# Moving the cast of the next rows behind the fourth eviction, one weight set for three expert tiles, and twelve weight pieces split early

## The chip, the cores and the metric

The kernel runs on one core of one Trainium2 chip. The metric is the device time of the core in microseconds (us). A core has TensorE (PE; its weight loads are listed apart as PEld), VectorE (DVE), ScalarE (ACT), GpSimd (POOL) and SyncE (SP), which here issues most DMAs. They run their own instruction streams and wait for each other on semaphores.

## The reference, cut to what matters

The kernel computes a spectral mixing layer and then a mixture of experts with one expert per token.

```python
# x: 8 sequences of 2496 tokens, 256 wide, float32
X = np.fft.rfft(x, axis=1)                 # over the sequence
Yr = Xr @ w_r - Xi @ w_i + b_r             # 256 x 256 mixing
Yi = Xr @ w_i + Xi @ w_r + b_i
Y = soft_threshold(Yr, 0.01) + 1j * soft_threshold(Yi, 0.01)
x = np.fft.irfft(Y, n=2496, axis=1).reshape(19968, 256)
logits = x @ w_gate + modality_bias[modality_id]      # 8 experts
e_idx = argmax(logits); gate = softmax(logits)[e_idx]
for e in range(8):                         # w1[e]: 256 x 1024, w2[e]: 1024 x 256
    out[e_idx == e] = gate * (relu(x[e_idx == e] @ w1[e]) @ w2[e])
```

## The kernel before, in words

The kernel has two parts, one after the other. The attention part (class `Attn`, with `Route`) transforms, mixes and transforms back the eight sequences in a loop over `b`; it writes each token's row, with its gate and token number, into a buffer in memory (`xs`) that is sorted by expert. GpSimd does that with indirect DMAs, the scatters. The expert part (class `Experts`) goes over `NF` = 78 tiles of `T` = 256 sorted rows.

TensorE multiplies in a float32 form that rounds its operands, so each operand is split in a rounded high half and a low half that holds the rest, and three products are added: high times high, low times high, high times low. For the expert weights the split is made by `SplitWeights`: 64 pieces (eight experts in rank order, eight pieces of 256 KB each) are loaded, ScalarE casts a piece to its high half (line 1165), VectorE subtracts it from the piece (line 1159), and a store of 512 KB writes both halves to a buffer in memory, `wsp` (line 1152). Each call of `sw.tick()` loads up to three pieces if rooms are free, stores those subtracted in the call before, subtracts those cast in the call before, and casts `n` pieces. In the attention part the rooms are nine borrowed tiles, and the calls lie in the last two sequences; in the expert part there are five rooms, and the calls lie in the second layer of a tile, two in tiles 0 to 2 and in odd tiles, one in the others.

An expert tile (`ffn`) has two layers. Its rows come by five DMAs (`load_x`, lines 867 and 868), four tiles ahead. VectorE turns them (`prep`, line 880) to `tr`; ScalarE casts `tr` to `xh` (line 883); GpSimd, or VectorE up to tile 5, subtracts to `xl` (line 884); VectorE converts the row numbers to `ix` (line 886). The first layer makes eight blocks of 128 features in four pairs, `p` = 0 to 3, with 12 matmuls a pair (line 905). After each pair ScalarE writes `hh`, the high half of the relu (line 907), and VectorE `hl`, the rest (line 908). The second layer (line 935) adds 24 matmuls for each half of 128 rows, three for each feature block `f`: `hh` twice and `hl` once. `prep` of the next tile is called by `between()` when `p` is 2, that is after the evictions of pairs 0 and 1 and ahead of those of pairs 2 and 3.

The weights of a tile are two loads of 2 MB from `wsp` (`load_w`, line 843), one for each layer, into one of two sets `wb[i % 2]`. Tiles 0 and 1 load without a condition; a later tile loads only when its expert differs from that of the tile that used the set before, by a flag of the table. The tiles take the expert-sorted list in the order of `ORDER`. The load of a tile waits for the stores of the ranks that it can have, and that of tile 1 also for the last scatter of the attention part (`rt.early`), since the second set lies over a tile that the scatters read.

The order on TensorE, ScalarE, VectorE and GpSimd is the order in which the program is written (a manual schedule). The order of SP's queue is set by a planner from the program's dependences and estimated times; it is a single queue, so that an instruction that waits holds up those behind it. Generators fill gaps: `tick()` of `Experts` takes a step of the late routing work after each pair and in the second layer, and `self.side` one of a few packed small tiles.

Of the kernel before, what the change touches and what calls it, by code (L numbers as in the profile page):

```python
# [12 lines left out]
I32 = mybir.dt.int32  # L13
# [8 lines left out]
SEQ = 2496  # L22
N1, N2, K1 = 39, 64, 20
D = 256
E = 8
# [12 lines left out]
NTOK = 8 * SEQ  # L38
T = 256
REG = NTOK + T  # L40
TH = T // 2
NF = -(-NTOK // T)
# [1 line left out]
PACK = 4  # L44
SIDE = NF + PACK
HALF = 1
AHEAD = 2
SURE = (NTOK - 2 * SEQ - E * (T - 1)) // T // 2 * 2
LEAST = -(-(NTOK - 2 * SEQ - E * (T - 1)) // T)
ORDER = np.arange(128)  # L50
ORDER[:SURE:2] = [*range(2, SURE, 2), SURE - 1]
ORDER[1:SURE:2] = [0, *range(1, SURE - 1, 2)]
ORDER[SURE:NF:2], ORDER[SURE + 1:NF:2] = np.arange(SURE, (SURE + NF) // 2), np.arange(NF - 1, (SURE + NF) // 2 - 1, -1)
BIG = float(1 << 20)


def shape_constants(nb):
# [84 lines left out]
class Attn:  # L142
# [204 lines left out]
    def turn(self, b, i):  # L347

        zt = self.wt.tile([128, 2, 16, 32], F32, tag="zt", name=f"zt_{b}_{i}")
        z = self.z.rearrange("p (a n) k r -> p a (n k r)", n=4)  # L350
        self.nc.vector.transpose(zt.rearrange("p c s e -> p (c s) e"), z[:, :, 32 * i:32 * i + 32])
        self.zt = (self.zt if i else []) + [zt]
# [438 lines left out]
class Experts:  # L791
# [44 lines left out]
    def load_w(self, i, layer):  # L836
        nc = self.nc
        if layer == 0 or i >= NF:
            self.e = self.reg(i, 1, E - 1)
            self.kw = dict(cond=self.reg(i, 2, 1), cond_hint=False) if 2 <= i < NF else {}  # L840
        row = self.wsp[bass.ds(self.e * 128, 128), :]
        w = self.weights(i)[layer]
        ins = nc.sync.dma_start(w.rearrange("p h c f -> p (h c f)").bitcast(F32),
                                row[:, layer * 4096:(layer + 1) * 4096], **self.kw)
        self.sw.part(ins, "the ranks that a tile can have are complete before its load")
        while self.ranks < E and (i >= SURE or self.ranks * LEAST <= E * ORDER[i]):
            assert len(self.sw.stores[self.ranks]) == 8, (i, self.ranks)
            for store in self.sw.stores[self.ranks]:
                self.rt.order(ins, store)
            self.ranks += 1  # L850
        return ins

    def weights(self, i):
        return self.wb[i % 2] if i < NF else self.wh[i]

    def load_x(self, i):
        nc = self.nc
# [18 lines left out]
    def prep(self, i):  # L876
        nc = self.nc
        t, g = self.xt[i]
        tr = self.tr.tile([128, 2, T], F32, tag="tr", name=f"tr_{i}")
        nc.vector.transpose(tr.rearrange("p c (t s) -> p c s t", t=32), t.rearrange("p (s c e) -> p c s e", c=2, e=32))  # L880
        xh = self.h[i % 2].tile([128, 2, T], F32R, tag="xh", name=f"xh_{i}")
        xl = self.h[i % 2].tile([128, 2, T], F32R, tag="xl", name=f"xl_{i}")
        nc.scalar.copy(xh, tr)  # L883
        (nc.gpsimd if i > 5 else nc.vector).tensor_sub(xl, tr, xh)  # L884
        ix = self.x.tile([128, 2], I32, tag="ix", name=f"ix_{i}")
        nc.vector.tensor_copy(ix, g[:, :, 1])  # L886
        return xh, xl, ix

    def ffn(self, i, xh, xl, ix, between):

        nc = self.nc
        w1, w2 = self.weights(i)
        hh = self.h[i % 2].tile([128, 8, T], F32R, tag="hh", name=f"hh_{i}")
        hl = self.h[i % 2].tile([128, 8, T], F32R, tag="hl", name=f"hl_{i}")
        for p in range(4):
            if p == 2:
                between()
                next(self.side, None)
            ps = self.hps.tile([128, 2, T], F32, tag="h", name=f"h_{i}_{p}")
            for q in range(2):  # L900
                f = 2 * p + q
                terms = ((0, xh), (0, xl), (1, xh)) if i else ((0, xh), (1, xh), (0, xl))
                ops = [(lo, c, x) for lo, x in terms for c in range(2)]
                for n, (lo, c, x) in enumerate(ops):
                    self.done = nc.tensor.matmul(ps[:, q, :], w1[:, lo, c, f * 128:(f + 1) * 128], x[:, c, :],  # L905
                                                 start=n == 0, stop=n == 5)
            nc.scalar.activation(hh[:, 2 * p:2 * p + 2, :], ps, AF.Relu)  # L907
            nc.vector.scalar_tensor_tensor(hl[:, 2 * p:2 * p + 2, :], ps, 0.0, hh[:, 2 * p:2 * p + 2, :],  # L908
                                           ALU.max, ALU.subtract)
            self.tick()  # L910
        next(self.side, None)
        if i + 2 < NF:
            self.load_w(i + 2, 0)
        y = self.ps.tile([128, 2, D], F32, tag="y", name=f"y_{i}")
        if i == NF - 1:

            y = [y[:, 0, :], self.ps.tile([128, 2, D], F32, tag="y", name=f"y_{i}_1")[:, 0, :]]
        else:
            y = [y[:, 0, :], y[:, 1, :]]
        o = self.x.tile([128, 2, D], F32, tag="o", name=f"o_{i}")  # L920

        def out(s):
            gate = self.xt[i][1][:, s, 0:1]
            if s:
                nc.vector.tensor_scalar_mul(o[:, s, :], y[s], gate)  # L925
            else:
                nc.scalar.mul(o[:, s, :], y[s], gate)  # L927
            self.put(ix[:, s:s + 1], o[:, s, :])

        for s in range(2):  # L930
            n = 0
            for f in range(8):
                a, l = hh[:, f, s * 128:(s + 1) * 128], hl[:, f, s * 128:(s + 1) * 128]
                for lhsT, lo in ((a, 0), (a, 1), (l, 0)):
                    nc.tensor.matmul(y[s], lhsT, w2[:, lo, f, :], start=n == 0, stop=n == 23)  # L935
                    n += 1
                if f % 4 == 3:
                    self.tick()
                if f == 2 and (s == 0 or i % 2 or i < 3):
                    self.sw.tick()  # L940
            if s == 0:
                next(self.side, None)
                if i == NF - 1:
                    out(0)
        if i < NF - 1:
            out(0)
        out(1)
# [117 lines left out]
    def tick(self):  # L1065
        next(self.late, None)

    def run(self, late):

        self.late = late  # L1070
        self.load_w(0, 0)
        self.load_x(0)
        self.load_x(1)
        self.load_w(0, 1)
        self.load_x(2)
        self.load_x(3)
        self.rt.grid2 = self.rt.load_grid(self.cp, "c_grid2", 4 * E + 2)

        self.rt.order(self.load_w(1, 0), self.rt.early)
        self.load_w(1, 1)  # L1080
        nxt = self.prep(0)
        for i in range(NF):
            cur, self.tile = nxt, i

            def between():
                nonlocal nxt
                if i + 1 < NF:
                    nxt = self.prep(i + 1)

            if i == 27:  # L1090
                self.side = self.pack()
            elif i == 42:
                self.side = self.half(SIDE)
            self.ffn(i, *cur, between)
            if i + 2 < NF:
                self.load_w(i + 2, 1)
            if i + 4 < NF:
                self.load_x(i + 4)
            if i == 20:
                self.side_pools()  # L1100
                self.load_pack()
            elif i in (21, 22, 23, 24):
                self.pack_weights(1, i - 21)
            elif i in (29, 30, 31, 32):
                self.pack_weights(2, i - 29)
            elif i in (38, 39):
                self.load_half(SIDE, (i - 38,))
        for _ in self.side:
            pass

        k = SIDE + HALF
        more = self.nc.values_load(self.rt.ti[k:k + 1, 3:4], min_val=0, max_val=1,  # L1112
                                   skip_runtime_bounds_check_because="a flag")
        with self.tc.If(more > 0):
            for i in range(k, SIDE + E):
                self.load_half(i)
                for _ in self.half(i):
                    pass


class SplitWeights:
# [47 lines left out]
        self.tc.declare_no_dep(ins.ins, group="wsp", reason=why)  # L1169
        self.tc.add_to_no_dep_group("wsp", ins.ins)  # L1170

    def tick(self, n=1, ranks=E):
        for _ in range(3):
            if self.free and self.todo and self.todo[0][0] < ranks:
                self.load()
                self.free -= 1
        self.store()
        self.rest()
        self.cast(n)
        self.now += 1  # L1180


def build(tc, I, out, nb):
    nc = tc.nc
    with ExitStack() as outer:
        dp = outer.enter_context(tc.tile_pool(name="wsp", bufs=1, space=DRAM))
        wsp = dp.tile([E * 128, 8192], F32, name="wsp")
        with ExitStack() as ctx:
# [116 lines left out]
            for b in range(nb):  # L1305
                folds, done = b + 2 < nb, b == nb - 1
                d = int(b == 0)
                for g in range(5):
# [8 lines left out]
                    if b == nb - 2 and g == 4:  # L1317
                        sw.begin(spare, 9)
                        sw.tick(0, AHEAD)
                    elif done:  # L1320
                        sw.tick((2, 2, 2, 2, 0)[g], AHEAD)
                    if b == 0:
# [170 lines left out]
```

## Time and profile before

| what | value |
|---|---|
| median of 3 runs | 1491.37 us (1487.02 to 1494.53) |
| profiled execution | 1491.51 us, span 1489.7 us |
| mean granted TensorE clock | 0.981 of full speed |
| TensorE busy | 1415.7 us, 95% of the span |
| VectorE, ScalarE, GpSimd busy | 50%, 39%, 37% |
| weight loads of the expert tiles | from 549.2 to 1476.1 us of the span |

Times of rows are counted from the start of the span. An idle time in square brackets stands before the instruction, with what ended it. Matmuls overlap, so the busy time of one is longer than the distance between two; the distance is read from the starts. The granted clock is 1.00 at 2.4 GHz and 0.50 at 1.2 GHz.

### The profile page before, as it was taken

How to read it: one execution, taken by the hardware profiler on the slowest of the kernel's cores; microseconds unless marked ns; L12 is line 12 of the kernel's file. 1: busy time of each engine (PE TensorE's matmuls, PEld its weight loads, DVE VectorE, ACT ScalarE, POOL GpSimd, SP SyncE). 2: the span in 40 equal slices, each digit the busy share in tenths (PEclk: the TensorE clock that was granted, in tenths of full speed). 3: DMA queues.
4: the chain of work that ended last, by engine and by line, in shares of the span. 5: the costliest groups of instructions: out<-in, count | busy, mean ns of one | idle time of the engine just before them, and what ended most of it. 6: DMA issues, size and time to landing. Idle time of an engine off the chain costs nothing. (4 is left out here: it accounts for less than half of the span.)

```text
span 1489.7 us, 34777 instructions
## 1 busy us (share of the span) xinstructions
PE 1415.7 (95%) x13058; PEld 1281.8 (86%) x13058; DVE 748.0 (50%) x1427; ACT 574.1 (39%) x1127; POOL 552.6 (37%) x562
## 2 busy tenths in 40 slices
PE   4899999999999987999999999999999999999996
PEld 1777686876868767999999989999999999999996
DVE  2666767667677863445544444433333333333332
ACT  2545555455554742333333333323222223222321
POOL 1012656656565464562222222322222232223221
PEclk7999999999999999999999999999999999999998
DMA  8736465464645597665555788724322222372510
GB/s 272 223 120 189 134 194 177 146 209 136 209 140 184 203 316 243 199 171 151 164 167 144 248 260 256 233 45 114 93 44 44 44 50 51 72 239 54 160 36 23
DMA packets 305163, 229.34 MB, mean 154 GB/s; under 512 B 203998, under 2 KB 259040, under 8 KB 302432
## 3 DMA queue, kind: packets, MB, share of 16 engines
q1 hardware_dynamic: 285120, 185.46, 43.9%
q0 software_dynamic: 19872, 41.61, 7.8%
q8 instruction: 105, 1.72, 0.5%
q14 instruction: 66, 0.54, 0.1%
HBM read 425.98 MB, written 112.54 MB: 361 GB/s over the span
## 5 line engine op out<-in xcount | busy, mean ns | idle before, releaser
L935 PE MATMUL y<-w,hh 128*128 128x256 f32 x2496 | 445.2, 279 | 0.1
L905 PE MATMUL h<-xh,w 128*128 128x256 f32 x2496 | 409.8, 281 | 13.7 <-DMA w<-wsp 10.8
L935 PEld LDWEIGHTS y<-w,hh 128*128 128x128 f32 x2496 | 380.3, 188 | 2.1 <-issue 1.7
L905 PEld LDWEIGHTS h<-xh,w 128*128 128x128 f32 x2496 | 345.2, 191 | 16.1 <-issue 11.5
L935 PE MATMUL y<-w,hl 128*128 128x256 f32 x1248 | 355.6, 285 | 2.8 <-DVE hl L908 0.9
L572 POOL DMA_INDIRECT xs<-x,si x256 | 258.4, 1009 | 186.2 <-ACT u L321 41.3
L908 DVE SCALAR_TENSOR_TENSOR hl<-h,hh 128x512 fp32r<-128x512 f32 x312 | 209.4, 689 | 232.7 <-ACT hh L907 232.6
L950 POOL DMA_INDIRECT out<-o,ix x157 | 154.1, 982 | 412.1 <-ACT o L927 378.2
L905 PE MATMUL h<-xl,w 128*128 128x256 f32 x1248 | 248.6, 281 | 0.0
L935 PEld LDWEIGHTS y<-w,hl 128*128 128x128 f32 x1248 | 234.0, 187 | 14.3 <-DVE hl L908 9.4
L907 ACT ACTIVATE hh<-h 128x512 fp32r<-128x512 f32 x312 | 178.2, 596 | 151.4 <-PE h L905 151.4
L905 PEld LDWEIGHTS h<-xl,w 128*128 128x128 f32 x1248 | 192.2, 191 | 0.0
L925 DVE TENSOR_SCALAR o<-y,xt 128x256 f32<-128x256 f32 x78 | 37.8, 485 | 306.3 <-ACT o L927 302.0
L884 POOL TENSOR_TENSOR xl<-tr,xh 128x512 fp32r<-128x512 f32 x72 | 93.0, 1292 | 202.1 <-ACT xh L883 202.1
L927 ACT ACTIVATE o<-y,xt 128x256 f32<-128x256 f32 x78 | 37.1, 475 | 320.8 <-PE y L935 320.8
L314 PE MATMUL mx<-wmix,Xh 128*128 128x256 f32 x640 | 106.4, 289 | 0.0
L883 ACT CAST xh<-tr 128x512 fp32r<-128x512 f32 x78 | 48.5, 622 | 143.4 <-DVE ix L886 131.9
L283 PE MATMUL s<-c_m,a 128*128 128x128 f32 x640 | 86.5, 279 | 12.7 <-DMA a<-scr 12.7
L314 PEld LDWEIGHTS mx<-wmix,Xh 128*128 128x128 f32 x640 | 87.4, 192 | 12.2 <-issue 7.3
L283 PEld LDWEIGHTS s<-c_m,a 128*128 128x128 f32 x640 | 82.6, 195 | 16.0 <-issue 11.7
L880 DVE STREAM_TRANSPOSE tr<-xt 128x512 f32<-128x512 f32 x78 | 90.8, 1164 | 0.1
L306 PE MATMUL mx<-wmix_r,Us 128*128 128x256 f32 x320 | 80.4, 393 | 4.5 <-DVE Us L292 4.5
(213 smaller groups left out, 1459.0 us busy)
## 6 DMA issues: line engine op xcount, KB each, us to landing
w<-wsp SPq DMA_DIRECT2D x156, 2048.0 KB
wsp<-wr SPq DMA_DIRECT2D x64, 512.0 KB
x<-in_x SPq DMA_DIRECT2D x40, 512.0 KB
a<-scr SPq DMA_DIRECT2D x80, 256.0 KB
xt<-xs SPq DMA_DIRECT2D x312, 64.0 KB
wr<-in_moe_w SPq DMA_DIRECT2D x64, 256.0 KB
scr<-ev SPq DMA_DIRECT2D x48, 240.0 KB
pw<-in_moe_w SPq DMA_DIRECT2D x8, 1024.0 KB
```

What stands on the lines that cost most here:

```text
L283: self.done = nc.tensor.matmul(ps[:, c, :, i, :], at[:, i, c * 128:(c + 1) * 128], self.m[:, k1 * 128:(k1 + 1) * 128].rearrange("p (r k) - ...
L306: nc.tensor.matmul(ps[:, 0, :], us[:, c, :], self.wr[:, c, :], start=False, stop=c == 1, skip_group_check=True)
L314: self.done = self.nc.tensor.matmul(ps[:, i, :], t[:, c, 1 - i, :], self.w[:, i, c, lo, :], start=False, stop=n == len(ops) - 1, skip_grou ...
L572: i = self.nc.gpsimd.indirect_dma_start(out=self.xs, out_offset=bass.IndirectOffsetOnAxis(ap=si[:, k:k + 1], axis=0), in_=rows, in_offset= ...
L880: nc.vector.transpose(tr.rearrange("p c (t s) -> p c s t", t=32), t.rearrange("p (s c e) -> p c s e", c=2, e=32))
L883: nc.scalar.copy(xh, tr)
L884: (nc.gpsimd if i > 5 else nc.vector).tensor_sub(xl, tr, xh)
L905: self.done = nc.tensor.matmul(ps[:, q, :], w1[:, lo, c, f * 128:(f + 1) * 128], x[:, c, :], start=n == 0, stop=n == 5)
L907: nc.scalar.activation(hh[:, 2 * p:2 * p + 2, :], ps, AF.Relu)
L908: nc.vector.scalar_tensor_tensor(hl[:, 2 * p:2 * p + 2, :], ps, 0.0, hh[:, 2 * p:2 * p + 2, :], ALU.max, ALU.subtract)
L935: nc.tensor.matmul(y[s], lhsT, w2[:, lo, f, :], start=n == 0, stop=n == 23)
L950: ins = self.nc.gpsimd.indirect_dma_start(out=self.out, out_offset=bass.IndirectOffsetOnAxis(ap=ix, axis=0), in_=o, in_offset=None, bounds ...
```

## The change

Three edits are made together.

1. `prep` is cut in two. The transpose and the index conversion stay at `p == 2` (`turn`). The cast to `xh` and the subtraction to `xl` (`split`) are called after the loop over `p`, so that on ScalarE they follow the fourth `hh`.
2. Tiles 0, 1 and 2 use weight set 0, tile 3 set 1, and then the sets alternate as before. Only tiles 0 and 3 load without a condition; tiles 1 and 2 don't load. The loads of tile 3 are issued in tile 0 (`load_ahead`), after its first and its second layer. An assertion states that the first four tiles lie in the full tiles of the largest expert.
3. The attention part loads 12 weight pieces in place of 16 (`AHEAD`, counted in pieces now and in ranks before); the other 52 are split in the expert part.

```diff
-AHEAD = 2
+AHEAD = 12
+assert max(ORDER[:4]) < -(-(NTOK - 2 * SEQ) // E) // T
...
     def load_w(self, i, layer):
-            self.kw = dict(cond=self.reg(i, 2, 1), cond_hint=False) if 2 <= i < NF else {}
+            self.kw = dict(cond=self.reg(i, 2, 1), cond_hint=False) if 4 <= i < NF else {}
...
     def weights(self, i):
-        return self.wb[i % 2] if i < NF else self.wh[i]
+        return self.wb[i % 2 if i > 1 else 0] if i < NF else self.wh[i]
+
+    def load_ahead(self, i, layer):
+        j = 3 if i == 0 else i + 2
+        if i == 1 or j >= NF:
+            return
+        ins = self.load_w(j, layer)
+        if i + layer == 0:
+            self.rt.order(ins, self.rt.early)
...
         nc.vector.transpose(tr.rearrange("p c (t s) -> p c s t", t=32), t.rearrange("p (s c e) -> p c s e", c=2, e=32))
+        ix = self.x.tile([128, 2], I32, tag="ix", name=f"ix_{i}")
+        nc.vector.tensor_copy(ix, g[:, :, 1])
+        return tr, ix
+
+    def split(self, i, tr, ix):
+        nc = self.nc
         xh = self.h[i % 2].tile([128, 2, T], F32R, tag="xh", name=f"xh_{i}")
         xl = self.h[i % 2].tile([128, 2, T], F32R, tag="xl", name=f"xl_{i}")
         nc.scalar.copy(xh, tr)
         (nc.gpsimd if i > 5 else nc.vector).tensor_sub(xl, tr, xh)
-        ix = self.x.tile([128, 2], I32, tag="ix", name=f"ix_{i}")
-        nc.vector.tensor_copy(ix, g[:, :, 1])
         return xh, xl, ix
...
     def ffn
             if p == 2:
-                between()
+                turn()
...
             self.tick()
+        split()
         next(self.side, None)
-        if i + 2 < NF:
-            self.load_w(i + 2, 0)
+        self.load_ahead(i, 0)
...
     def run
-        self.rt.order(self.load_w(1, 0), self.rt.early)
-        self.load_w(1, 1)
-        nxt = self.prep(0)
+        nxt = self.split(0, *self.prep(0))
...
-            self.ffn(i, *cur, between)
-            if i + 2 < NF:
-                self.load_w(i + 2, 1)
+            self.ffn(i, *cur, turn, split)
+            self.load_ahead(i, 1)
...
-    def tick(self, n=1, ranks=E):
+    def tick(self, n=1, upto=8 * E):
         for _ in range(3):
-            if self.free and self.todo and self.todo[0][0] < ranks:
+            if self.free and self.todo and 8 * E - len(self.todo) < upto:
```

## Rows read from the trace of the kernel before

**Rows 1.** Head of the page.

```profile
span 1489.7 us, 34777 instructions
```

**Rows 2.** Costliest groups: busy us, mean ns | idle before, what ended it.

```profile
L905 PE MATMUL h<-xh,w 128*128 128x256 f32 x2496 | 409.8, 281 | 13.7 <-DMA w<-wsp 10.8 <-ACT xh L883 2.9
...
L935 PEld LDWEIGHTS y<-w,hl 128*128 128x128 f32 x1248 | 234.0, 187 | 14.3 <-DVE hl L908 9.4
```

**Rows 3.** Stages: length, PE, PEld, DVE, ACT, POOL busy (count), clock, DMA share, GB/s.

```profile
585.10:770.00 184.90, 182.72 (x1540) 179.74 (x1539) 93.33 (x217) 65.47 (x121) 76.53 (x73) 1.00 0.61 173
770.00:798.70 28.70, 25.51 (x193) 25.21 (x193) 10.32 (x17) 8.09 (x15) 6.53 (x6) 0.88 0.47 115
...
1110.80:1464.90 354.10, 353.50 (x2978) 348.39 (x2977) 131.52 (x217) 101.68 (x186) 101.07 (x93) 1.00 0.32 81
```

**Rows 4.** Order of time in one tile, VectorE, ScalarE, GpSimd: start, length, instruction.

```profile
1160.80 1.14 DVE L880 STREAM_TRANSPOSE tr<-xt 128x512 f32<-128x512 f32 x1
...
1161.98 0.62 ACT L883 CAST xh<-tr 128x512 fp32r<-128x512 f32 x1 [1.82 <-DVE ix L886]
...
1162.50 1.08 ACT L907 ACTIVATE hh<-h 128x512 fp32r<-128x512 f32 x2
1162.68 1.29 POOL L884 TENSOR_TENSOR xl<-tr,xh 128x512 fp32r<-128x512 f32 x1 [2.83 <-ACT xh L883]
1163.13 0.69 DVE L908 SCALAR_TENSOR_TENSOR hl<-h,hh 128x512 fp32r<-128x512 f32 x1 [1.18 <-ACT hh L907]
```

**Rows 5.** Order of time, weight loads of that tile and the next.

```profile
1156.52 0.30 PEld L905 LDWEIGHTS h<-xh,w 128*128 128x128 f32 x2
...
1161.97 0.30 PEld L935 LDWEIGHTS y<-w,hh 128*128 128x128 f32 x2
...
1163.33 0.30 PEld L935 LDWEIGHTS y<-w,hh 128*128 128x128 f32 x2
1163.87 0.19 PEld L935 LDWEIGHTS y<-w,hl 128*128 128x128 f32 x1 [0.24 <-DVE hl L908]
1163.98 0.32 PEld L935 LDWEIGHTS y<-w,hh 128*128 128x128 f32 x2
...
1167.88 0.30 PEld L905 LDWEIGHTS h<-xh,w 128*128 128x128 f32 x2
...
1173.53 0.31 PEld L935 LDWEIGHTS y<-w,hh 128*128 128x128 f32 x2
...
1174.94 0.30 PEld L935 LDWEIGHTS y<-w,hh 128*128 128x128 f32 x2
1175.37 0.19 PEld L935 LDWEIGHTS y<-w,hl 128*128 128x128 f32 x1
```

**Rows 6.** Order of time, weight loads at the end of tile 16 and in tile 17.

```profile
755.08 0.19 PEld L935 LDWEIGHTS y<-w,hl 128*128 128x128 f32 x1
...
758.60 0.31 PEld L905 LDWEIGHTS h<-xh,w 128*128 128x128 f32 x2
...
764.04 0.30 PEld L935 LDWEIGHTS y<-w,hh 128*128 128x128 f32 x2
```

**Rows 7.** Order of time, TensorE, first matmuls of tiles 0 and 1.

```profile
549.19 1.22 PE L905 MATMUL h<-xh,w 128*128 128x256 f32 x4 [2.92 <-ACT xh L883]
...
571.84 0.77 PE L905 MATMUL h<-xh,w 128*128 128x256 f32 x2 [7.58 <-DMA w<-wsp]
```

**Rows 8.** Tile 1: length, weight loads busy (count), clock, DMA share, GB/s.

```profile
571.80:585.10 13.30, 12.84 (x96) 0.86 0.82 284
```

**Rows 9.** Order of time, SP's queue, weight loads from memory of tiles 1 and 2.

```profile
563.68 2.23 SPq L843 DMA_DIRECT2D w<-wsp  x3
```

**Rows 10.** Five us of the attention part, columns as in rows 3.

```profile
510.00:515.00 5.00, 5.00 (x52) 4.55 (x52) 4.64 (x10) 4.05 (x9) 3.17 (x3) 1.00 0.97 339
```

**Rows 11.** Order of time, VectorE, the last subtraction of a piece there.

```profile
530.72 0.68 DVE L1159 TENSOR_TENSOR wr<-wr 128x512 fp32r<-128x512 f32 x1
```

**Rows 12.** Order of time, SP's queue, a weight load for tile 19.

```profile
784.69 0.09 SPq L843 DMA_DIRECT2D w<-wsp  x1
```

More of the change, by code (lines that the diff above doesn't have):

```diff
@@ L884, in prep, with ffn @@
         (nc.gpsimd if i > 5 else nc.vector).tensor_sub(xl, tr, xh)
-        ix = self.x.tile([128, 2], I32, tag="ix", name=f"ix_{i}")
-        nc.vector.tensor_copy(ix, g[:, :, 1])
         return xh, xl, ix
-    def ffn(self, i, xh, xl, ix, between):
+    def ffn(self, i, xh, xl, ix, turn, split):
         nc = self.nc
@@ L1077, in run, with turn @@
         self.rt.grid2 = self.rt.load_grid(self.cp, "c_grid2", 4 * E + 2)
-        self.rt.order(self.load_w(1, 0), self.rt.early)
-        self.load_w(1, 1)
-        nxt = self.prep(0)
+        nxt = self.split(0, *self.prep(0))
         for i in range(NF):
             cur, self.tile = nxt, i
-            def between():
+            def turn():
                 nonlocal nxt
@@ L1088, in between, with split @@
                     nxt = self.prep(i + 1)
+            def split():
+                nonlocal nxt
+                if i + 1 < NF:
+                    nxt = self.split(i + 1, *nxt)
             if i == 27:
```

## The prediction

> **What bounds the kernel now.** The page's head gives the span [rows 1]; the profiled execution took 1491.51 us, so 1.8 us lie outside the span, and the median of the runs shown, 1491.37 us, is the same time within 0.01%. The sum below is made against 1491.51. What a measurement of this kernel can tell from no change is about 0.5%, or 7.5 us.
>
> I read the costliest groups first, for TensorE's idle time. Two groups of the expert part stand out: the first matmul of a tile waits 10.8 us in all for weights from memory (in two places, as will be seen), and the weight loads of the second layer wait for `hl` [rows 2]. The second looks small, 14.3 us over the whole kernel, but weight loads overlap, so idle time shows only what exceeds that overlap; the wait has to be read from the starts. Then the table of stages: TensorE is at 25 of 25 us nearly everywhere, and yet 31 consecutive tiles take 354.1 us with 2977 weight loads, 96 to a tile, which is 11.42 us a tile; the 16 tiles from 585.1 us take 11.56 [rows 3]. So I asked which of these 11.42 us are matmul and which are wait.
>
> One tile in order of time [rows 4] shows the chain. VectorE turns the next rows for 1.14 us after the second `hl`, converts the indices, and only then ScalarE casts `xh` (1161.98). The third and fourth `hh` stand behind this cast on ScalarE and start at 1162.50, though the matmuls of the third pair ended near 1160.9 (36 x 0.1135 after 1156.52, and 0.28 for the last one, as the groups of [rows 2] have it); the third `hl` runs 1163.13 to 1163.82. TensorE's row shows who pays: in the second layer the third weight load of feature block 4, the first that reads this `hl`, starts at 1163.87, 0.54 us after the two before it, where two normally take 0.23: a hole of 0.31 us. In the next tile it is 0.43 against 0.24: 0.19 us [rows 5]. The next tile waits for the chain in every tile I followed that no side work delays.
>
> The same rows show a second thing. The cadence has two levels. The first layer is 48 matmuls: it takes 5.45 us in one tile (0.1135 each) and 5.65 in the next (0.1177), all at a granted clock of 1.00. After the hole the tile of 1156.52 runs at the slower level. But the level need not change where nothing waits: [rows 6] show a tile end at the fast one (31 loads in 3.52 us, 0.1135) and the next go through its first layer at it (48 in 5.44, 0.1133).
>
> At the head of the expert part TensorE waits 2.92 us for the first `xh`, then stands 7.58 us until the weights of tile 1 land [rows 7], and works through tile 1 at a mean granted clock of 0.86, that is partly at 1.2 GHz in place of 2.4 [rows 8]. Those weights were issued at 563.68 [rows 9], behind all x loads, and landed 8.2 us later.
>
> **The change, part by part.** *The cast after the fourth eviction.* Removed: one cast of 0.62 us that stands ahead of two evictions on ScalarE. What is late next is VectorE: transpose and index conversion stay between the second and third `hl`, so the third `hl` can start when `xh` did, at 1161.98, instead of 1163.13, and end at 1162.67; it is wanted at 1163.33 + 2 x 0.1135 = 1163.56. Cover of 0.9 us: the hole closes. The fourth `hl`, with `hh` from about 1162.3 (the second layer starts at 1161.97, the last matmul of the first ends 0.28 later), ends near 1163.65 and is wanted at 1161.97 + 20 x 0.1135 = 1164.24; 0.6 us to spare. The moved cast then runs 1162.9 to 1163.5, GpSimd's subtraction (1.29 us) to about 1164.9, and the next tile starts at 1167.88: three us of cover, cost nothing. If that cover were gone each us late would cost a us per tile. Behind the moved cast on ScalarE stand only a weight piece's cast and the output scaling.
>
> How much a closed hole gives depends on the cadence, which no row of a tile without a hole fixes, so it is bounded. All matmuls at the slow level: 96 x 0.1177 = 11.30, a gain of 0.12 a tile. All at the fast level: 96 x 0.1133 = 10.88, a gain of 0.54. Of tiles 2 to 77 I count 70 that have the hole (six are delayed by inserted work or the jam below). The 16 early tiles have 0.14 more to give (VectorE's routing steps and, up to tile 5, its own subtraction lengthen their chain), 2.2 us. Gains: 70 x 0.12 + 2.2 = 10.6 us, or 70 x 0.54 + 2.2 = 40 us. Taking only the hole away and leaving the mix of levels (0.25 x 70 + 2.2) gives 20. I take 29, between the unchanged mix and all fast, because the level changes in these rows where TensorE has waited, and the fast one is carried over a tile's end.
>
> The Trainium skill, in "TensorE: Matmul & The Clock Gate", section "Back-to-back issue gap", gives for a lone warm matmul of N columns N / 2.4 plus 2.5 ns, which is 109 ns at 256 columns. The rows here show nothing under 113; by that section of the skill a tile would take 10.5 us and this part would give 68.
>
> *One weight set for three tiles.* The first four tiles take tiles 2, 0, 4, 1 of the list, all of the largest expert, so nothing but the buffer changes. The loads for tile 1 (two of 2 MB) become those of tile 3, issued after the first layer of tile 0; the conditional loads of tiles 2 and 3 go, which moved no data. The stall of 7.58 us goes, for tile 1's rows are in place by then. With it goes the half clock: tile 1 takes 13.30 us for its 96 loads [rows 8] against 11.42, so 1.9 more. The 2.92 us before tile 0 stay: they hang on the chain copy, transpose, cast, which is not touched. What is late next is tile 3's weights. It would start near 549.2 + 15 + 2 x 11.3 = 586.8 (tile 0 runs to 564.3, where the stall begins). If they are issued no later than tile 1's were (563.68, still behind the last scatter), the same 8.2 us make it 572 for the first layer: 15 us to spare. Gain 9.5 us; bounds 7.6 (the clock stays low) and 12.4 (the 2.92 goes too).
>
> *Twelve pieces, not sixteen, in the attention part.* Four loads of 256 KB, four casts (0.62 by `xh`, of the same shape), four subtractions (0.68) and four stores of 512 KB move behind it. In the attention part TensorE is at 5.00 of 5.00 in a stretch where they lie [rows 10], so ScalarE's 2.5 and VectorE's 2.7 us are mostly hidden there; the subtraction at 530.72 [rows 11] sits right ahead of a copy for which TensorE waits, at most 0.7 us. On SP the loads that must wait for a room to come free, pieces 9 to 15, become 9 to 11. Between nothing and 1.5 us I take 0.5. In the expert part the pieces keep their rate, about three in two tiles. Four more casts and subtractions lie in slack of 0.6 us and more, each once. Counted in program order, rank 1 is stored in the second half of tile 3 and first asked for in tile 4, for tile 6, so a late store has 17 us of cover; the later ranks have more.
>
> Sum: 29 + 9.5 + 0.5 = 39; 1491.5 - 39 = 1452.5, called 1452.
>
> **The rivals.** *The slow level throughout.* Without a hole nothing may kick TensorE out of it. For it: the tails after both holes of [rows 5] are slow. Against: the first layers there are at different levels, so a tile's start changes it too. Gain 10.6 + 10 = 20.6: 1471; the case covers 1464 to 1473.
>
> *The fast level throughout.* For it: [rows 6]. 40 + 10 = 50: 1441.5; it covers 1437 to 1444.
>
> *A cadence under any row.* The load right behind a hole follows at 0.11 us (1163.87 to 1163.98 in [rows 5]). Should all matmuls come to that, each ns under 113.3 is worth 96 x 70 = 6.7 us: 22 us under the fast case, 1419. Against: the loads after that one are back at 0.118, and the fast level holds 0.1133 for 48 in a row. The formula of the Trainium skill named above would put this case near 1414.
>
> *The wait moves into SP's queue.* In tile 18 a fence, a store that waits for VectorE, and x loads stand in that queue ahead of a weight load that has nothing to move; it is issued at 784.69 [rows 12], and TensorE, which waits for it, loses the other 3.2 of the 10.8 us. Two tiles take 28.7 us from 770 on, 5.9 more than 2 x 11.42, at a mean clock of 0.88 [rows 3]. SP's order comes from a planner, so such a jam may move, go, or come twice. One more costs 6 us, one fewer gives 6. Two or three more, with the slow level, leave 1473 to 1487.
>
> *Slower than before.* Tile 3's weights get stuck in that queue behind stores of pieces that wait for tile 2. From issue at 578.6 on, tile 3 waits us for us, plus 2 for the clock. To use up even the slow level's 20 us and 7.5 more, the issue would have to slip to about 604; nothing before shows such a slip for a load without a condition.
>
> **How the numbers follow.** Forecast (hole closed, levels mixed, stall gone; 1444 to 1464): 0.55. Slow level: 0.22. Fast level: 0.11. Under any row: 0.02. Jams: 0.07, of which 0.04 within 0.5% and the rest faster. Slower: 0.03. So faster 0.93, same 0.04, slower 0.03. The range 1437 to 1473 leaves out the jams, the slower case and the lowest one, 0.12, and would leave out 0.23 if it stopped above the fast case.
>
> **What would show it.** In the profile after: the hl loads of block 4 follow at 0.12 us like the others; `hh` three and four start as their matmuls end; tile 1 starts right behind tile 0 near 564, at full clock; 31 late tiles take 337 to 350 us. Wrong would be: loads still waiting for `hl` (then VectorE's transpose sets the chain), a wait for weights at tile 3, or a longer jam.

## Result and profile after

The changed kernel takes 1444.93 us (median of 4 runs, 1444.1 to 1447.13), the kernel before 1490.28 beside it (4 runs, 1487.02 to 1494.53): ratio 0.970, 95% interval 0.9675 to 0.9721, or 45 us less. 1452 was forecast, with 1437 to 1473 as the range. The profiled execution of the changed kernel took 1447.13 us with a span of 1445.4, against 1489.7 in [rows 1]: 44.3 us less. The starts of the tiles' first weight loads say where they lie:

| stage | before | after | gain |
|---|---|---|---|
| start of span to tile 2 | 585.15 | 574.66 | 10.49 |
| tiles 2 to 17 | 184.80 | 176.44 | 8.36 |
| tiles 18 and 19 | 28.81 | 28.31 | 0.50 |
| tiles 20 to 26 | 79.70 | 76.34 | 3.36 |
| tiles 27 to 43 (inserted small tiles) | 209.48 | 205.61 | 3.87 |
| tiles 44 to 76 | 376.97 | 359.82 | 17.15 |
| the rest | 24.79 | 24.22 | 0.57 |

The stages in the table of windows answer to [rows 3]; the third is 31 tiles in both:

```profile
574.66:751.10 176.44, 175.79 (x1540) 175.69 (x1539) 106.22 (x217) 67.17 (x121) 76.99 (x73) 1.00 0.63 177
751.10:779.41 28.31, 24.72 (x195) 24.55 (x193) 12.36 (x17) 8.31 (x15) 6.54 (x6) 0.88 0.50 127
1083.17:1421.18 338.01, 338.01 (x2978) 338.01 (x2977) 129.00 (x217) 104.82 (x186) 101.22 (x93) 1.00 0.34 85
```

31 tiles take 338.01 us, 10.90 each, in place of 11.42, and PEld's busy time fills the stretch to the last hundredth. Tiles 18 and 19 take nearly as long as before (28.31 for 28.81) at the same mean clock, 0.88.

The costliest groups of the changed kernel, which answer to [rows 2]:

```profile
L948 PE MATMUL y<-w,hh 128*128 128x256 f32 x2496 | 431.5, 277 | 1.9 <-DMA w<-wsp 1.9
L918 PE MATMUL h<-xh,w 128*128 128x256 f32 x2496 | 403.6, 279 | 6.1 <-DMA w<-wsp 3.6 <-ACT xh L898 2.5
...
L948 PEld LDWEIGHTS y<-w,hl 128*128 128x128 f32 x1248 | 234.3, 188 | 0.0
```

The 14.3 us of idle time ahead of the loads of `hl`, 9.4 of them put down to VectorE's `hl`, are 0.0. Of 10.8 us for weights in the first layer 3.6 are left, all in the jam at tile 19; 1.9 us stand at a new place, the second layer.

Tile 50 in order of time, VectorE, ScalarE and GpSimd first, as in [rows 4], then the weight loads, as in [rows 5]:

```profile
1131.09 1.16 DVE L889 STREAM_TRANSPOSE tr<-xt 128x512 f32<-128x512 f32 x1
...
1131.21 0.60 ACT L920 ACTIVATE hh<-h 128x512 fp32r<-128x512 f32 x1 [0.76 <-PE h L918]
...
1132.08 0.17 DVE L891 CAST ix<-xt 128x2 int32<-128x2 f32 x1
1132.09 0.69 DVE L921 SCALAR_TENSOR_TENSOR hl<-h,hh 128x512 fp32r<-128x512 f32 x1
...
1132.57 0.60 ACT L920 ACTIVATE hh<-h 128x512 fp32r<-128x512 f32 x1 [0.76 <-PE h L918]
...
1133.06 0.62 ACT L898 CAST xh<-tr 128x512 fp32r<-128x512 f32 x1
```

```profile
1126.78 0.30 PEld L918 LDWEIGHTS h<-xh,w 128*128 128x128 f32 x2
...
1132.26 0.30 PEld L948 LDWEIGHTS y<-w,hh 128*128 128x128 f32 x2
...
1133.62 0.30 PEld L948 LDWEIGHTS y<-w,hh 128*128 128x128 f32 x2
1133.85 0.19 PEld L948 LDWEIGHTS y<-w,hl 128*128 128x128 f32 x1
...
1137.70 0.31 PEld L918 LDWEIGHTS h<-xh,w 128*128 128x128 f32 x2
```

`hh` three and four (1131.21, 1132.57) start when their matmuls end, the third `hl` right behind the index conversion. It ends at 1132.78 and is wanted at 1133.85, 1.07 us later. The `hl` load of block 4 follows at 0.23 us like the others (0.54 in [rows 5]). The tile takes 10.92 us, its first layer 5.48, which is 0.114 a matmul; behind the place of the former hole it is 0.113 (34 loads in 3.85 us).

The start, which answers to [rows 7 to 9]: the first matmul of tile 0 on TensorE, and SP's queue with the fence (L619), the stores of pieces (L1167) and the weight loads (L844).

```profile
550.01 1.22 PE L918 MATMUL h<-xh,w 128*128 128x256 f32 x4 [2.46 <-ACT xh L898]
```

```profile
518.46 0.38 SPq L619 DMA_DIRECT2D xs<-pad  x1
519.11 1.90 SPq L1167 DMA_DIRECT2D wsp<-wr  x3
523.86 0.37 SPq L844 DMA_DIRECT2D w<-wsp  x1
...
552.56 0.34 SPq L844 DMA_DIRECT2D w<-wsp  x1
...
557.49 0.34 SPq L844 DMA_DIRECT2D w<-wsp  x1
```

Tile 1 starts at 563.20, 0.11 us behind the last load of tile 0, and takes 11.46 us, as against 13.30 [rows 8]. But SP's queue is 11 us earlier as well: the first weights of tile 3 are issued at 552.56, where those of tile 1 were issued at 563.68 [rows 9]. Nothing in the forecast says so.

And one wait is new. SP's queue and TensorE at tile 31, the first behind tile 3 that loads another expert into set 1:

```profile
893.98 1.07 SPq L1167 DMA_DIRECT2D wsp<-wr  x2
...
896.00 0.37 SPq L844 DMA_DIRECT2D w<-wsp  x1
896.95 12.79 SPq L876 DMA_DIRECT2D xt<-xs  x4
```

```profile
913.02 0.47 PE L948 MATMUL y<-w,hh 128*128 128x256 f32 x2 [1.94 <-DMA w<-wsp]
```

The second layer's weights are issued at 896.00 and TensorE goes on at 913.02, 17 us later; the DMA engines are full in that stretch (busy share 0.95 and more from 895 to 910). The same load and the first matmul that reads it, in the kernel before:

```profile
918.31 0.37 SPq L843 DMA_DIRECT2D w<-wsp  x1
```

```profile
935.07 0.39 PE L935 MATMUL y<-w,hh 128*128 128x256 f32 x2
```

There the load had 16.65 us until the first weight load of that layer (934.96), and TensorE didn't wait. In the changed kernel 14.8 are left. Tile 30 and the first layer of tile 31 take 16.33 us in place of 16.95, which is 0.6 less. The other 1.2 are SP's queue: behind two stores of pieces (893.98) and a load of one it comes to the weights 1.53 us after the start of tile 30 (894.47), where it came 0.30 after it (918.01).

### The profile page after: what moved, and what is told of

Its sections match the earlier page's. It is cut to its first block, busy times and chain, and to the rows that moved or that the text cites. A ratio compares the mean times of both kernels' runs of the same rounds, so it can differ in the third digit from the quotient of the medians.

```text
span 1445.4 us, 34758 instructions
## 1 busy us (share of the span) xinstructions
PE 1379.8 (95%) x13058; PEld 1258.2 (87%) x13058; DVE 776.3 (54%) x1427; ACT 581.5 (40%) x1127; POOL 553.5 (38%) x562
## 5 line engine op out<-in xcount | busy, mean ns | idle before, releaser
L948 PE MATMUL y<-w,hh 128*128 128x256 f32 x2496 | 431.5, 277 | 1.9 <-DMA w<-wsp 1.9
L918 PE MATMUL h<-xh,w 128*128 128x256 f32 x2496 | 403.6, 279 | 6.1 <-DMA w<-wsp 3.6
L918 PEld LDWEIGHTS h<-xh,w 128*128 128x128 f32 x2496 | 340.2, 189 | 8.2 <-issue 4.2
L948 PE MATMUL y<-w,hl 128*128 128x256 f32 x1248 | 345.5, 277 | 0.0
L921 DVE SCALAR_TENSOR_TENSOR hl<-h,hh 128x512 fp32r<-128x512 f32 x312 | 215.1, 690 | 165.2 <-ACT hh L920 163.8
L920 ACT ACTIVATE hh<-h 128x512 fp32r<-128x512 f32 x312 | 186.6, 598 | 255.7 <-PE h L918 255.7
L918 PE MATMUL h<-xl,w 128*128 128x256 f32 x1248 | 245.5, 278 | 0.0
L323 DVE SCALAR_TENSOR_TENSOR s<-mx,u 128x512 f32<-128x512 f32 x80 | 55.2, 691 | 52.0 <-ACT u L322 51.4
```

Of the source, the lines that this page charges most:

```text
L323: nc.vector.scalar_tensor_tensor(s, ps, LAM, u, ALU.add, ALU.min)
```

## Experiments

**Each edit by itself.** Three kernels carry one edit each, a fourth the first two. All four ran on a second chip, on which the attention part takes about 50 us longer (tile 0 starts near 600) and the kernel before 1533.69 us (1526.78 to 1537.25, 19 runs). The expected times were worked out from the first measurement, so only gains can be compared with them.

Only the cast moved:

```diff
             if p == 2:
-                between()
+                turn()
...
             self.tick()
+        split()
```

> The cast moved behind the fourth eviction and nothing else. Theory: the holes close, TensorE then keeps the fast cadence, and this edit alone gives the tiles from 2 on what they gained with all three edits (the starts of tiles 2 and 77 lie 586.5 us... before 879.8 and after 846.5 us apart, 33 us): 1457 us, with 31 late tiles at 338 us. Rival: closing the holes gives only the holes (about 20 us) and the fast cadence is owed to the lighter traffic of the other two edits: 1470 us, 31 late tiles near 347 us.

Measured: 1495.72 us (1494.44 to 1501.8), ratio 0.9768, interval 0.9729 to 0.9807: 38 us less. Most of tiles 2 to 76 take 10.89 or 10.92 us; longer are those with inserted work, a few others (11.1 to 11.3), the jam at tiles 18 and 19 (27.96 together) and tile 31 (12.23, so that the wait for its weights comes with the cast alone). No load of `hl` waits for VectorE any more:

```profile
L940 PEld LDWEIGHTS y<-w,hl 128*128 128x128 f32 x1248 | 234.3, 188 | 0.7 <-issue 0.6
```

Only the weight set:

```diff
-        return self.wb[i % 2] if i < NF else self.wh[i]
+        return self.wb[i % 2 if i > 1 else 0] if i < NF else self.wh[i]
+
+    def load_ahead(self, i, layer):
+        j = 3 if i == 0 else i + 2
+        if i == 1 or j >= NF:
+            return
...
```

> One weight set for the first three tiles and nothing else. Theory: the stall of 7.6 us ahead of tile 1 and the half clock behind it go, 9.5 to 11 us: 1480 us; the holes stay at 0.2 to 0.3 us a tile. Rival: tile 3 waits for its weights in place of tile 1, and the gain is under 3 us: 1488 us or more.

Measured: 1533.22, ratio 0.9992 (0.9974 to 1.0011). On this chip nothing was there to be removed: in the kernel with the cast alone, where the old weight sets stand, tile 1 follows tile 0 without a wait. The tiles keep their holes, 11.2 to 11.5 us.

Only twelve pieces:

```diff
-AHEAD = 2
+AHEAD = 12
-    def tick(self, n=1, ranks=E):
+    def tick(self, n=1, upto=8 * E):
```

> Twelve pieces in place of sixteen in the attention part and nothing else. Theory of the prediction: TensorE covers the four casts and subtractions, 0.5 us gained: 1490 us, and tile 1 still waits for its weights. Rival: the shorter queue on SP lets the weights of tile 1 be issued some 10 us earlier, so that this edit alone takes away the stall ahead of tile 1 too: 1481 us.

Measured: 1527.84 (1521.77 to 1531.0), ratio 0.997 (0.995 to 0.999), 5.9 us less. Tile 0 starts at 596.16 here and at 600.76 to 602.53 in the three other kernels on this chip, which split sixteen pieces there; so by one profile of each, most of the 5.9 us lie ahead of tile 0. On the other chips no such difference shows: tile 0 starts at 545.95 to 550.01 in seven profiles with twelve pieces, and at 547.85 to 549.19 in three with sixteen.

The first two edits together:

> The first two edits together, sixteen pieces still split in the attention part. Theory: as the whole change, 1445 to 1447 us, since the third edit is worth 0.5 us. Rival: without the shorter queue on SP the weights of tile 3 or the rows of the first tiles come late, and a part of the start's gain is lost: 1450 us or more.

Measured: 1496.12, ratio 0.9759 (0.9728 to 0.9791), the cast's gain and nothing more. What follows from the four: the cast alone gives 38 us, and what the other two give had to be measured where the wait at tile 1 exists.

**The two small edits where the wait exists.** The same kernels on a chip that ran the kernel before in 1490.31 us (1487.78 to 1491.51, 7 runs).

> The weight set alone, once more. Theory: it gives what TensorE waits for at tile 1 in the kernel before on the same chip. Where that is 7.6 us with a tile 1 of 13.3 us behind it, as in the first profile, the gain is 9 to 11 us, ratio about 0.993; where the attention part takes 600 us and there is no wait, nothing. Rival (the wait moves to tile 3's weights): tile 3 starts late by what tile 1 no longer waits, ratio 1.00 on either.

> Twelve pieces alone, once more. Seven stores of pieces (9.9 us of SP's queue) stand ahead of the first tile's loads in the kernel before, three (1.9 us) in the changed one, and its loads for tile 3 are issued at 552.6 us where those for tile 1 were at 563.7. Theory: this edit moves SP's queue, so that it alone takes most of the wait for tile 1's weights away where there is one: gain 5 to 8 us, ratio 0.995 to 0.997, and the gains of the two edits don't add. Rival (the last scatter holds these loads, not the queue): they are issued as late as before, gain 0 to 1 us.

Measured: the weight set alone 1478.39 (ratio 0.9918, 0.9901 to 0.9935), twelve pieces alone 1478.36 (0.9919, 0.9903 to 0.9936). Each gives 12 us, both more than their theories said, and the gains don't add: all three edits give 45 to 47 us, while 38, 12 and 12 would be 62. Most of what is missing is a gain that either edit brings and that counts once. SP's queue tells why, here that of the kernel with the weight set alone and then that with twelve pieces alone:

```profile
520.56 0.49 SPq L619 DMA_DIRECT2D xs<-pad  x1
521.31 10.35 SPq L1157 DMA_DIRECT2D wsp<-wr  x7
534.86 0.38 SPq L844 DMA_DIRECT2D w<-wsp  x1
```

```profile
517.40 0.38 SPq L618 DMA_DIRECT2D xs<-pad  x1
518.06 1.88 SPq L1152 DMA_DIRECT2D wsp<-wr  x3
523.13 0.37 SPq L843 DMA_DIRECT2D w<-wsp  x1
...
552.14 3.63 SPq L843 DMA_DIRECT2D w<-wsp  x3
```

With sixteen pieces seven stores stand between the fence and the first tile's weights, with twelve three; the whole queue behind them is 11.7 us earlier (3.2 of that already at the fence, the rest behind it), and tile 1's weights, issued at 552.14, are there when tile 0 ends at 561.29. Either edit takes the 7.58 us away.

**Is it the wait for the transpose, or the cast's own time?** The kernel before, with the transpose and the index conversion one pair earlier and the cast left where it was, ahead of the third eviction:

```diff
         for p in range(4):
+            if p == 1:
+                turn()
             if p == 2:
-                between()
+                split()
```

> The kernel before, with only this changed: the transpose of the next rows and the index conversion come one pair earlier (after the first eviction); the cast stays ahead of the third eviction. Theory (ScalarE's wait for the transpose holds the third eviction up, not the 0.62 us of the cast itself): with the rows turned by then, the cast fits between the second and the third eviction, the hole at the third hl closes, all tiles run at 0.1133 us a matmul (10.89 us a tile), and the gain is that of the moved cast, 33 to 38 us, ratio 0.975 to 0.978. Rival (any work ahead of the third eviction costs): the hole stays in part, tiles of 11.1 to 11.3 us, gain 10 to 20 us, ratio 0.987 to 0.993.

Measured: 1451.8 us (1451.05 to 1452.74) beside 1491.18 of the kernel before on that chip (1490.0 to 1493.23, 7 runs); ratio 0.9737 (0.9721 to 0.9753), 39.4 us less. Every tile from 44 to 76 takes 10.89 to 10.92 us, and the group of `hl` loads in its profile waits for nothing:

```profile
L941 PEld LDWEIGHTS y<-w,hl 128*128 128x128 f32 x1248 | 234.3, 188 | 0.0
```

So the cast's 0.62 us ahead of the third eviction costs nothing. What cost was that it stood there waiting for VectorE. Moving the cast is one way out, having its input ready is another, of about the same worth (38 and 39.4 us, on two chips).

**What does a short wait cost?** The changed kernel, with the transpose done twice (1.14 to 1.16 us more on VectorE), so that the 1.07 us of cover are just used up:

```diff
         nc.vector.transpose(tr.rearrange("p c (t s) -> p c s t", t=32), t.rearrange("p (s c e) -> p c s e", c=2, e=32))
+        nc.vector.transpose(tr.rearrange("p c (t s) -> p c s t", t=32), t.rearrange("p (s c e) -> p c s e", c=2, e=32))
```

> The changed kernel, with the transpose done twice in each tile, so that VectorE has 1.14 us more to do between the second and the third hl. The cover of the third hl in the changed kernel is 1.06 us by its trace, so this uses it up and leaves it about 0.1 us late. Theory (the cadence of 0.1133 us a matmul is owed to TensorE's waiting for nothing inside a tile): a hole of only 0.1 us is enough to throw tiles back to a mix with 0.1177, so a tile takes 11.1 to 11.4 us in place of 10.89 and the kernel is 15 to 40 us slower than the changed one, ratio to the kernel before 0.98 to 0.997. Rival (only the waiting itself costs): 0.1 us in 70 tiles, about 8 us over the changed kernel, ratio about 0.975.

Measured: 1473.83 us (1469.43 to 1475.06), ratio 0.9875 (0.9855 to 0.9895); the changed kernel beside it took 1444.22 (1443.68 to 1445.42), so 29.6 us more. The weight loads of tile 51 of that kernel:

```profile
1153.43 0.31 PEld L919 LDWEIGHTS h<-xh,w 128*128 128x128 f32 x2
...
1158.89 0.30 PEld L949 LDWEIGHTS y<-w,hh 128*128 128x128 f32 x2
...
1160.25 0.30 PEld L949 LDWEIGHTS y<-w,hh 128*128 128x128 f32 x2
1160.64 0.19 PEld L949 LDWEIGHTS y<-w,hl 128*128 128x128 f32 x1
...
1164.50 0.30 PEld L919 LDWEIGHTS h<-xh,w 128*128 128x128 f32 x2
```

A hole of 0.16 us (0.39 for 0.23). This tile stays at the fast level and takes 11.07, which is 10.90 and the hole. It is a rare one: over tiles 44 to 76 the mean hole is 0.15 us and the mean tile 11.34, 0.43 above the changed kernel. So 0.28 of the 0.43 is not waiting but matmuls at 0.1177 in place of 0.1133, as the distances of the weight loads have it: 73% of them are at the slow level, 3% in the changed kernel. The rival, waiting alone, allowed 8 us of the 29.6; with the hole of 0.15 us that came it would be 10.

The same with half a transpose, inside the cover:

```diff
+        nc.vector.transpose(tr.rearrange("p c (t s) -> p c s t", t=32)[:, :, :4], t.rearrange("p (s c e) -> p c s e", c=2, e=32)[:, :, :4])
```

> The changed kernel with half a transpose more in each tile, 0.57 us of VectorE's time between the second and the third hl by half the time of a whole one. Theory (cost only past the cover of 1.06 us): half of the cover is left, the tiles stay at 10.89 us, ratio to the kernel before as for the changed one, 0.969, within 0.2%. Rival (more work there costs in proportion, a whole transpose cost 29.6 us): about 15 us more than the changed kernel, ratio 0.978.

Measured: 1445.75 (1444.3 to 1449.97), ratio 0.9712 (0.969 to 0.9733), against 0.9687 (0.9671 to 0.9703) for the changed kernel on another chip; the intervals overlap. The tiles settle it: 44 to 76 take 10.89 to 10.92, as without it. From the start of the transpose to that of the third `hl` it is 1.00 us in the changed kernel, 1.71 with the half transpose and 2.19 with the whole one. So 0.71 us of work inside the cover of 1.07 is free, and 0.48 more than that costs about 28.

**The jam and tile 31.** The changed kernel again, and a version of it in which the calls that split pieces are issued behind the last load of rows on SP's queue and tiles 28 to 30 split none (`gates` is the last DMA of `load_x`):

```diff
-                if f == 2 and (s == 0 or i % 2 or i < 3):
-                    self.sw.tick()
+                if f == 2 and (s == 0 or i % 2 or i < 3) and i not in (28, 29, 30):
+                    with self.tc.issue_after(self.gates.ins):
+                        self.sw.tick()
```

> The changed kernel once more, beside the three others. Theory: tiles of 10.89 us as in its first run; ratio 0.969 where the chip's attention part takes 549 us and TensorE waits for the weights of tile 1 in the kernel before, about 0.973 where it takes 600 us and there is no such wait (38 us of the cast and 6 of the twelve pieces of 1533, nothing of the weight set).

> The changed kernel, with two things more: each call that splits weight pieces in the expert part is issued behind the last load of rows on SP's queue, so that a store that waits for VectorE no longer stands ahead of the loads of rows for tile 20 and the weight load of tile 19; and tiles 28 to 30 split no pieces, so that the stores don't share the memory with the weights of tile 31. Theory: the jam of tiles 18 and 19 (about 6 us) and the wait for weights in tile 31 (2.3 us) go, the kernel is 6 to 8 us under the changed one, ratio to the kernel before about 0.965. Rival (the jam is set by the fence for the last sorted rows, not by the store): it only moves, no gain, ratio as for the changed kernel.

Measured: the changed kernel 1444.22 as above, ratio 0.9687; the new version 1436.24 (1432.93 to 1436.98), ratio 0.9633 (0.9617 to 0.9649): 8 us less. The jam in the changed kernel's first profile, on SP, VectorE and TensorE, and then the stretch of tiles 18 and 19 in the new version's windows:

```profile
750.53 0.43 SPq L619 DMA_DIRECT2D xs<-pad  x1
760.05 0.37 SPq L1167 DMA_DIRECT2D wsp<-wr  x1
761.00 2.94 SPq L876 DMA_DIRECT2D xt<-xs  x4
...
765.65 0.11 SPq L844 DMA_DIRECT2D w<-wsp  x1
```

```profile
758.12 1.80 DVE L1174 TENSOR_TENSOR wr<-wr 128x512 fp32r<-128x512 f32 x1
```

```profile
765.88 0.76 PE L918 MATMUL h<-xh,w 128*128 128x256 f32 x2 [3.59 <-DMA w<-wsp]
```

```profile
745.38:767.18 21.80, 21.80 (x194) 21.80 (x193) 12.35 (x17) 8.32 (x15) 6.53 (x6) 1.00 0.64 181
```

The store at 760.05 has waited for a subtraction that ends at 759.92. Behind it stand the loads of rows and then a weight load that has nothing to move, at 765.65; TensorE goes on 0.2 us later, at a granted clock of 0.50 until about 771. With the pieces behind the rows the two tiles take 21.80 us in place of 28.31, at full clock. Tile 31 takes 10.89 there, against 13.27 and 14.97 in the two profiles of the changed kernel.

The first half of that version alone:

> The first half of the version that came out 8 us under the changed kernel: the calls that split pieces are issued behind the last load of rows on SP's queue, but tiles 28 to 30 split pieces again. Theory: tiles 18 and 19 take 10.9 us each as in that version, tile 31 waits for its weights as in the changed kernel (2 to 4 us); so 5 to 6 us under the changed kernel, ratio about 0.965. Rival: the pause was what counted for both, ratio 0.969.

Measured, on the chip of the two small edits: 1439.8 (1438.07 to 1442.82), ratio 0.967 (0.9652 to 0.9688), an interval that meets the changed kernel's; by its trace tiles 18 and 19 take 21.81 us together and tile 31 takes 13.09. So the order on SP frees the jam and the pause frees tile 31; the total time alone would not have told it.

## Why the prediction was near, step by step

*The hole closes: right.* The signs named came, with 1.07 us of cover where 0.9 was worked out. One reading of the rows was loose: the 14.3 us of idle time ahead of the `hl` loads [rows 2] are not all a wait for `hl`, which is named for 9.4; the sum doesn't use that figure.

*How much it gives: the term that was mis-sized.* 29 us were taken, between 20 for an unchanged mix of levels and 40 for all fast. Two measurements give 38 (cast alone) and 39.4 (transpose earlier); in the changed kernel's first profile the tiles from 2 on gain 33.8, since new waits take a part back. By the tile, [rows 3] against 338.01 / 31: 11.42 less 10.90 is 0.52; the mean hole in tiles 44 to 76 of the kernel before is 0.26, near the 0.25 of [rows 5], and the other half is cadence, since 68% of its weight loads there are at the slow level. 0.52 x 70 + 2.2 is 38.6. The case that came is the rival "the fast level throughout", at 0.11 chance. The argument for it stood in the text (the level changes where TensorE has waited, and the fast one is carried over a tile's end): followed to its end it gives all fast once nothing waits, not a value half way. By the Trainium skill, "TensorE: Matmul & The Clock Gate", section "Back-to-back issue gap", a lone warm matmul of 256 columns takes about 109 ns, an estimate by a formula that the section gives for a lone matmul and not for a stream of weight loads and matmuls like this one. The traces don't show 109: with no wait at all the distance stays at 113.3.

*The total fell inside the forecast's own case, 1444 to 1464, at its lower edge, and that is in part luck:* the cadence was that of the other case, and things that the sum left out took some of it back. The fast case was worked out as 1441.5, with 40 us from tile 2 on; the first profile has 33.8 there. Tile 31's new wait costs 2.4. Tiles 2 to 17 gave 8.4 where that case has 10.8 (16 x 0.54 + 2.2): tile 9 takes 12.12 in both kernels, and two tiles behind it 11.3. Three more tiles behind inserted work take 11.3 too. The lead of a transfer was worked out for tile 3, where 15 us were to spare (and tile 3 doesn't wait), but not for the later change of expert, whose weights had 16.65 us before and took 17. How much of that wait the faster tiles make, and how much SP's queue, the other kernels show: with the cast alone the lead is 15.9 us and the wait 1.1, with the early transpose 16.0 and 0.3.

*One weight set, 9.5 us: right.* Alone it gives 12 us of the kernel's time; up to tile 2 its profile gains 9.6 (585.15 to 575.57), and 1.4 of the rest lie in the jam (27.44 for 28.81). Tile 1 at full clock is worth 1.84 (13.30 to 11.46), where 1.9 was put.

*Twelve pieces, 0.5 us: the wrong engine was costed.* ScalarE, VectorE and TensorE were looked at, and SP only for the pieces that wait for a room. SP's queue had seven stores, 9.9 us, between the fence and the first tile's loads. Alone the edit gives 12 us because that queue holds tile 1's weights. Beside the weight set there is less left: tile 2 starts at 574.66 and 570.86 in two profiles of the changed kernel, and at 575.57 with the weight set alone, 1 to 5 us. The two edits together are best read against the kernel with the early transpose, which has the old start, on the same chip: the changed kernel's second profile gains 12.7 us up to tile 2 (583.60 to 570.86) and loses 4.6 in tiles 27 to 43, at tile 31 and the two behind it (14.97, 11.30 and 11.31 for 11.19, 10.92 and 10.89). Whether the work of the four pieces itself was worth 0.5 us in the attention part can't be told: the start of tile 0 differs by 4 us between two profiles of the changed kernel.

*Jams and slower:* tiles 18 and 19 took 28.31 for 28.81, no more and no fewer jams; tile 3's weights were early, not late.

What stays open: why the level changes. The traces show only when. In the changed kernel all tiles that begin slow come behind inserted work or a wait, and within two tiles the level is fast again. That a hole brings the slow level is shown by taking holes away and putting them back; by what means it does so is not.

## What to carry to other kernels

Where a stream of matmuls is fed just in time, price a short wait by the whole tile behind it and not by its own length: holes of 0.15 us cost 0.43 us a tile here, and the cure (38 us) was worth twice the holes that it took away (0.26 in each of 70 tiles, 18 us). An engine that waits in the middle of its order holds up all that is queued behind it, so either move it behind, or have its input ready. When a loop gets shorter, work out anew the lead of every transfer that was timed by it, and what stands ahead of it in the DMA queue; and when work leaves a stage, count its stores in that queue too.

## What the runs showed that was not expected

Weight loads and matmuls of this shape keep one of two distances, 113.3 or 117.7 ns, both at a granted clock of 1.00. In tiles 44 to 76, with a hole in every tile 68 to 73% are slow, without a hole 3%, in the kernel with the early transpose as in the changed one.

TensorE's half clock (1.2 GHz) at the start of tile 0, behind about 3 us of idle time (2.92 and 3.04), did not last equally long: from tile 0's first matmul to 555 us the mean granted clock was 0.50 in the kernel before and 0.75 with the weight set alone.

One chip took about 50 us longer for the attention part than the others and ran the expert tiles at the same pace, 10.89 us. The traces don't show why.
